# Feature chunks loaded by two transfers each, and the stores of split weight sums moved from SyncE's queue to GpSimd's

## The chip, the cores and the metric

One NeuronCore of a Trainium2 chip runs the whole program. The metric is the device time of one execution in microseconds (us): 3232.86 us is the median of three executions of the kernel before, which lie between 3230.33 and 3237.58 us.

## The reference

The input x is 2048 x 576, all in float32. The kernel computes

```
xn = layernorm(x)
s  = softmax_attention(xn @ wqkv, 32 heads of 18) @ wo
g  = silu( ((relu(x' @ W_gate)) * (x' @ W_up)) @ W_down )      # x' = xn, F = 4608
out = x + s * g
```

(in the code of the reference: `xn = _layernorm(x); s = _A_ref(xn, ...); g = _silu(_B_ref(xn, W_gate, W_up, W_down)); return x + s * g`). Products are made at nearly float32 accuracy: each operand is split into a high part (a float32r copy) and a low part (the difference), and three of the four part products are summed.

## The kernel before, in words

**Stages.** First a projection stage: the 2048 rows are taken in four groups of 512 (`g`), normalized, transposed to features, split into high and low parts, and multiplied with the weights of q, k and v. The results go to DRAM (`qd`, `kd`, `vd`). The split features go to DRAM too, as `xTd`, by `spill`. Then come 144 units: four row groups times 36 blocks of 128 of the 4608 hidden features. Unit `k` (function `emit_unit`) multiplies the 576 features of its row group with one gate and one up block (`up`, 27 steps of matmuls, tile `pg`). Steps of attention are woven between them: from unit 0 the row maxima (`pm`, reduced by VectorE on L272), from unit 16 also the exponentials (`psx`, then ScalarE). After every odd unit, 64 matmuls of `attend` (tile `po`) follow. After every even unit, `down` or `down_made` multiplies the hidden features of two units with the down weights (tile `py`). So work comes in pairs of units, and the groups of 64 `po` matmuls mark the pace. At last a stage projects with `wo` and writes the result.

**The features.** A chunk is 64 features x 512 rows as high and low parts. It stands twice in a tile of 128 partitions, on partitions 0 to 63 and on 64 to 127, because the gate product uses the lower and the up product the upper half of the array. The pool `xA` has nine buffers, one for each of the nine chunks of a group, so the next group's chunk can come only when the last unit of the present group (units 35, 71, 107) is done with that chunk. `load_x` (L298) loads one; `half` calls it after each chunk of these units, and the stage ahead calls it for group 0. Its DMA is issued on SyncE's queue (SP) and is pinned in program order there. Row loads of the weights (`rg`), of keys and queries (`kq`, `kA`, `qT`), the store of attention results (`od`) and others share SP's queue. In the units up to 17, SP's DMAs keep the program's order (`sp.kept`); after that a planner places them by its own estimates, except what is pinned.

**The sums of weight blocks.** From unit 36 on, the down product uses seven products of sums of blocks (as in Strassen's scheme), and these sums of the weights are made once, in units 1 to 35, and read back later (`load_w`, 378 loads of tile `w`). `make_items` builds, for each of 18 pairs of blocks, one load (`wp`) and seven items. An item has three parts: `start` adds two blocks into `wt` (VectorE in units 1 to 15, GpSimd after), `middle` copies it as the high part into `ws` on ScalarE (L773, `copy_now`), and `end` subtracts on GpSimd for the low part and stores the tile to `wtd`. `make_step` runs `end` of one item, `middle` of the next and `start` of a third. There are three such steps in each of the units 1 to 15 and five in each of the units 16 to 35. `ws` and `wt` have two buffers each, so ScalarE's copy of an item waits until the store of the item two before it has landed. ScalarE works in order: behind that copy stand the exponentials that free TensorE's banks.

**GpSimd's own order.** GpSimd (POOL; every instruction of it passes L88 and is kept in program order) also splits the gate and up weights of the next unit (`gw`, a copy and a subtraction), the down weights (`dw`), the hidden features (`hh`), and adds sums (`y`, `c`). In the kernel before it issues only the DMAs of `qd`, `kd`, `vd` in the first stage and of `gd` at the end of each group.

Of the kernel before, what the change touches and what calls it, by code (L numbers as in the profile page):

```python
# [9 lines left out]
F32 = mybir.dt.float32  # L10
# [9 lines left out]
def kernel(  # L20
# [10 lines left out]
    nc = tc.nc  # L31
    P = 128
    R = P // 2
# [39 lines left out]
    def vec(i):  # L73
        return tc.keep_in_program_order(i)

    pinned = tc.keep_in_program_order
# [28 lines left out]
    gp = Kept(nc.gpsimd)  # L105
    sp = Maybe(nc.sync, True)
# [13 lines left out]
    xTd = dram.tile([NQ, XC, P, 2 * 512], F32, name="xTd")  # L120
    gd = dram.tile([S, D], F32, name="gd")
    od = dram.tile([D, S], F32, name="od")
    wtd = dram.tile([NF // 2, 7, P, 2, HC], F32, name="wtd")
# [41 lines left out]
    def xtile(pl):  # L165
        return pl.tile([P, 2, 512], F32R, tag="x", name="x")
# [131 lines left out]

    def load_x(g, c):
        xc = xtile(xA)  # L300
        pinned(
            nc.sync.dma_start(
                xc.rearrange("p a s -> p (a s)").bitcast(F32),
                xTd[g, c // 2, c % 2 * R : c % 2 * R + R].unsqueeze(0).to_broadcast([2, R, 1024]),
            )
        )
        xcur.setdefault(g, []).append(xc)

    with ExitStack() as st:
# [293 lines left out]
        for g in range(NQ):  # L603
# [46 lines left out]
            if last:  # L650
# [17 lines left out]
                for c in range(KC - 2, KC):  # L668
                    load_x(0, c)
            else:  # L670
                for j in range(4):
                    v_job(wv, g, j)
                    if j == 0 and g == 0:
                        nxt = load_rows(g + 2)
                    if j == 1:
                        spill(g, marks[-1] if g == 0 else None)
                    if j and g == NQ - 2:
                        for c in range(3 * j - 3, min(3 * j, KC - 2)):
                            load_x(0, c)
# [28 lines left out]
    def up(k):  # L708

        g, f = units[k]  # L710
        gw = gus.pop(k)
        if k < N1 and (k % 2 == 0 or k == N1 - 1):
            ps = [psO.tile([P, 512], F32, name="po"), shared("pg2")]
        else:
            ps = [bank("pg0"), bank("pg1")]
        last = f == NF - 1 and k + 1 < len(units)
        xg = xcur[g]

        def ops(t, c, i, j, rows):
            return gw[rows, i, c, :], xg[c][rows, j, :]  # L720

        def half(t):
            for n, _ in enumerate(row_half(ps[t], ops, t)):
                c = n // len(PRODUCTS)
                if t and n % len(PRODUCTS) == 2:
                    if last:
                        load_x(units[k + 1][0], c)
                        if c == KC - 1:
                            load_up(k + 2)
                    elif k + 1 == len(units):  # L730
                        run_tasks(hooks.get(c, []))
                yield

        return ps, [half(t) for t in range(2)]
# [37 lines left out]
    def copy_now(dst, src):  # L772
        after(nc.scalar.activation(dst, src, AF.Copy), newest[0])  # L773
# [175 lines left out]
    def make_items(fp):  # L949

        st = {}

        def load():
            st["w"] = pw.tile([P, 2, D], F32, name="wp", bufs=1)
            for i in range(2):
                f = 2 * fp + i
                sp.dma_start(st["w"][:, i], wd[f * P : (f + 1) * P, :])

        def start(m, on):
            w = st["w"]  # L960
            b = [[w[:, i, c * HC : (c + 1) * HC] for c in range(2)] for i in range(2)]
            x0, x1, op = {
                0: (b[0][0], b[1][1], ALU.add), 1: (b[0][0], None, None), 2: (b[0][1], b[1][1], ALU.subtract),
                3: (b[1][0], b[0][0], ALU.subtract), 4: (b[1][1], None, None), 5: (b[0][0], b[0][1], ALU.add),
                6: (b[1][0], b[1][1], ALU.add),
            }[m]
            if op is not None:
                t = pw.tile([P, HC], F32, name="wt")
                if on is nc.vector:
                    vec(on.tensor_tensor(t, x0, x1, op))  # L970
                else:
                    gp.tensor_tensor(t, x0, x1, op)
                x0 = t
            st[m] = x0, pw.tile([P, 2, HC], F32R, name="ws")

        def middle(m):
            x0, s_ = st[m]
            copy_now(s_[:, 0], x0)

        def end(m):  # L980
            x0, s_ = st.pop(m)
            gp.tensor_tensor(s_[:, 1], x0, s_[:, 0].bitcast(F32), ALU.subtract)
            sp.dma_start(wtd[fp, m], s_.bitcast(F32))

        return [(load, start, middle, end, m) for m in (None, 1, 4, 0, 2, 3, 5, 6)]

    for fp in range(NF // 2):
# [432 lines left out]
```

## Time and profile before

| what | value |
|---|---|
| median of the three runs shown | 3232.86 us |
| time of the profiled execution | 3239.11 us |
| its span, first to last instruction | 3237.3 us |
| mean granted TensorE clock | 0.914 |
| TensorE busy | 2772.1 us (86%) |
| VectorE busy | 1867.7 us (58%) |
| ScalarE busy | 1665.0 us (51%) |
| GpSimd busy | 1746.8 us (54%) |
| SP's DMA queue | 350.43 MB, 37.6% of 16 engines |
| GpSimd's DMA queue | 27.66 MB, 2.5% of 16 engines |

The span and the busy times are of the one profiled execution; its own time is 1.8 us more than its span. A granted clock of 1.0 is 2.4 GHz and of 0.5 is 1.2 GHz. The chain of waits is followed back from the last instruction; here it reaches back to 683 us and not further, so the time before that is read from other views. "SPq" is SyncE's queue, and the time of a DMA there is that of its issue, not of its transfer.

### The profile page before, as it was taken

The page shows a single profiled execution, that of the slowest core. Times are in us where ns is not written, and L with a number is a line of the kernel's source. Part 1 is how long each engine was busy: PE and PEld are TensorE (multiplying, and loading weights), DVE is VectorE, ACT ScalarE, POOL GpSimd, SP SyncE. Part 2 cuts the span into 40 slices and gives each one's busy share as a digit, 9 for nine tenths or more (in the row PEclk, how much of TensorE's full clock was granted, in tenths as well). Part 3 has the DMA queues.
Part 4 walks back from the last instruction along what each step waited for, and adds up shares of the span by engine and source line. Part 5 has one row for each costly group of instructions (what it writes and reads, how often), then busy time and mean ns, then how long its engine had stood idle before and what let it go on. Part 6 is the DMA issues. An engine that isn't in the chain of part 4 may idle for free.

```text
span 3237.3 us, 63467 instructions
## 1 busy us (share of the span) xinstructions
PE 2772.1 (86%) x24653; PEld 2047.1 (63%) x24653; DVE 1867.7 (58%) x3118; ACT 1665.0 (51%) x3761; POOL 1746.8 (54%) x1762
## 2 busy tenths in 40 slices
PE   9967777787783799999992799999992799999999
PEld 8856665565662567767761567767771567766668
DVE  5233445554552577777771477777770577777315
ACT  3211114454442467767761467666671467767662
POOL 4225555555542465665650655656651665656667
PEclk9978878898886899999995899999995899999999
DMA  8454444344331433343331343443341334343346
GB/s 269 179 176 116 128 116 123 105 122 119 117 105 70 135 104 107 109 119 106 107 108 62 102 119 105 113 117 108 99 113 66 107 112 111 104 121 93 91 124 217
DMA packets 324979, 382.14 MB, mean 118 GB/s; under 512 B 33480, under 2 KB 214472, under 8 KB 324680
## 3 DMA queue, kind: packets, MB, share of 16 engines
q1 hardware_dynamic: 316936, 350.43, 37.6%
q0 software_dynamic: 7744, 27.66, 2.5%
q8 instruction: 195, 3.19, 0.4%
q14 instruction: 104, 0.85, 0.1%
HBM read 293.78 MB, written 83.69 MB: 117 GB/s over the span
## 4 chain that ended last, share of the span: by engine, by line
PE 54%; DMA 10%; POOL 7%; ACT 4%; issue 3%; SPq 1%; DVE 0%; POOLq 0%; ACTq 0%; DVEq 0%
PE pg L70 17%; PE po L70 11%; PE py L70 11%; PE pm L70 7%; PE psx L70 6%; DMA x<-xTd 6%; DMA wtd<-ws 2%; POOL gw L88 2%; PE pw L70 2%; POOL y L88 2%; ACT p L100 1%; SPq L100 1%; DMA rg<-in_B_W_up_dram 1%; ACT hc L773 1%; ACT hd L773 1%
## 5 line engine op out<-in xcount | busy, mean ns | idle before, releaser
L272 DVE TENSOR_REDUCE mx<-pm 128x1 f32<-128x512 f32 x2048 | 1345.0, 687 | 790.4 <-PE pm L70 647.3
L70 PE MATMUL pg<-x,gw 64*128 64x512 f32 x7533 | 1495.0, 410 | 171.8 <-DMA x<-xTd 153.4
L100 ACT ACTIVATE p<-psx 128x512 f32<-128x512 f32 x2048 | 1102.9, 615 | 405.7 <-PE psx L70 337.3
L70 PEld LDWEIGHTS pg<-x,gw 64*128 64x128 f32 x7533 | 1062.0, 195 | 302.8 <-DMA x<-xTd 165.9
L70 PE MATMUL po<-p,va 128*32 128x512 f32 x4096 | 454.3, 595 | 0.0
L88 POOL TENSOR_TENSOR gw<-rg,gw 128x1152 fp32r<-128x1152 f32 x131 | 349.4, 2667 | 10.5
L88 POOL TENSOR_TENSOR c<-add,c 128x288 f32<-128x288 f32 x204 | 157.8, 807 | 344.0 <-ACT add L890 344.0
L70 PEld LDWEIGHTS po<-p,va 128*32 128x32 f32 x4096 | 126.3, 110 | 294.8 <-issue 283.7
L70 PE MATMUL psx<-qT,kq 56*128 56x512 f32 x608 | 231.9, 410 | 33.9 <-ACT p L100 32.2
L70 PE MATMUL pm<-kq,qT 54*128 54x512 f32 x608 | 240.3, 417 | 19.1 <-ACT p L100 19.1
L70 PE MATMUL psx<-kq 56*128 56x512 f32 x512 | 199.7, 414 | 49.1 <-ACT p L100 47.6
L88 POOL CAST gw<-rg 128x1152 fp32r<-128x1152 f32 x131 | 150.7, 1151 | 168.3 <-PE pm L70 98.2
L88 POOL TENSOR_TENSOR hr<-h 128x256 f32<-128x256 f32 x108 | 79.4, 735 | 289.7 <-DVE nm L1099 151.0
L70 PE MATMUL pm<-kA,kq 54*128 54x512 f32 x512 | 207.2, 426 | 31.1 <-DMA kA<-kd 18.9
L70 PE MATMUL pm<-kq 54*128 54x512 f32 x512 | 207.2, 424 | 18.4 <-DVE mx L272 13.3
L70 PE MATMUL psx<-kq,kA 56*128 56x512 f32 x512 | 193.5, 406 | 20.5 <-ACT p L100 19.1
L70 PE MATMUL psx<-qT,kA 56*128 56x512 f32 x416 | 166.7, 423 | 45.2 <-ACT p L100 44.3
L70 PE MATMUL pm<-kA,qT 54*128 54x512 f32 x416 | 165.5, 422 | 12.6 <-ACT p L100 12.6
L742 DVE TENSOR_TENSOR h<-pg,h 128x512 f32<-128x512 f32 x144 | 98.1, 681 | 132.2 <-ACT h L100 132.2
L890 ACT ACTIVATE add<-py 128x288 f32<-128x288 f32 x357 | 141.3, 411 | 61.2 <-PE py L70 26.5
L773 ACT ACTIVATE ws<-wt 128x288 fp32r<-128x288 f32 x90 | 39.7, 442 | 254.3 <-DMA wtd<-ws 216.8
L70 PE MATMUL py<-dw,hh 64*128 64x288 f32 x1728 | 145.6, 327 | 25.9 <-DVE mx L272 12.9
(139 smaller groups left out, 4427.6 us busy)
## 6 DMA issues: line engine op xcount, KB each, us to landing
w<-wtd SPq DMA_DIRECT2D x378, 288.0 KB
rg<-in_B_W_gate_dram SPq DMA_DIRECT2D x131, 288.0 KB
rg<-in_B_W_up_dram SPq DMA_DIRECT2D x131, 288.0 KB
wtd<-ws SPq DMA_DIRECT2D x126, 288.0 KB
x<-xTd SPq DMA_DIRECT2D x36, 512.0 KB
rd<-in_B_W_down_dram SPq DMA_DIRECT2D x36, 288.0 KB
wp<-in_B_W_down_dram SPq DMA_DIRECT2D x36, 288.0 KB
qd<-hh POOLq DMA_DIRECT2D x16, 512.0 KB, 6.9
```

What stands on the lines that cost most here:

```text
L70: newest[0] = tc.keep_in_program_order(nc.tensor.matmul(*args, **kw))
L88: return lambda *args, **kw: tc.keep_in_program_order(op(*args, **kw))
L100: i = op(*args, **kw)
L272: vec(nc.vector.tensor_reduce(mx[:, h, b, j, c : c + 1], ps, axis=AX.X, op=ALU.max))
L742: vec(nc.vector.tensor_tensor(h, ps[1], h, ALU.mult))
L773: after(nc.scalar.activation(dst, src, AF.Copy), newest[0])
L890: pinned(nc.scalar.activation(src, outs_[p][j], AF.Copy))
```

## The change

Two edits. `load_x` issues two DMAs a chunk, each of which fills 64 partitions from the same block of `xTd`, where one DMA with a broadcast source of leading size 2 filled all 128. And `end` of an item stores its tile from GpSimd's queue in place of SP's.

```
     def load_x(g, c):
         xc = xtile(xA)
-        pinned(
-            nc.sync.dma_start(
-                xc.rearrange("p a s -> p (a s)").bitcast(F32),
-                xTd[g, c // 2, c % 2 * R : c % 2 * R + R].unsqueeze(0).to_broadcast([2, R, 1024]),
+        for t in range(2):
+            pinned(
+                nc.sync.dma_start(
+                    xc[t * R : (t + 1) * R].rearrange("p a s -> p (a s)").bitcast(F32),
+                    xTd[g, c // 2, c % 2 * R : c % 2 * R + R],
+                )
             )
-        )
         xcur.setdefault(g, []).append(xc)
...
         def end(m):
             x0, s_ = st.pop(m)
             gp.tensor_tensor(s_[:, 1], x0, s_[:, 0].bitcast(F32), ALU.subtract)
-            sp.dma_start(wtd[fp, m], s_.bitcast(F32))
+            gp.dma_start(wtd[fp, m], s_.bitcast(F32))
```

## Rows read from the trace of the kernel before

**Rows 1.** The page: TensorE's busy tenths in 40 slices of the span.
```profile
PE   9967777787783799999992799999992799999999
```
**Rows 2.** The chain of waits, in order of time: start us, us, what.
```profile
980.12 37.07 DMA wtd<-ws x2
1036.44 34.98 DMA x<-xTd
...
1696.49 56.86 DMA x<-xTd x2
...
2429.48 90.34 DMA x<-xTd x3
```
**Rows 3.** The waits, whole span: us in total, times, longest.
```profile
ACT ws L773 <- DMA wtd<-ws: 228.9, 49, 19.0
...
PE pg L70 <- DMA x<-xTd: 153.4, 19, 10.0
...
PE po L70 <- DMA x<-xTd: 17.7, 2, 9.9
```
**Rows 4.** Windows: length, busy us (instructions) by engine, granted clock, DMA share, GB/s.
```profile
2440.00:2450.00 10.00, 2.50 (x9) 1.48 (x9) 1.38 (x2) 1.01 (x2) 0.00 (x0) 0.50 0.13 52
1106.00:1107.00 1.00, 1.00 (x12) 0.82 (x9) 0.96 (x3) 1.00 (x3) 0.14 (x1) 1.00 0.95 273
...
180.00:220.00 40.00, 16.28 (x105) 13.70 (x107) 8.43 (x14) 2.43 (x7) 11.85 (x10) 0.62 0.57 171
```
**Rows 5.** TensorE in order of time: three `po` groups, units 31 to 37.
```profile
890.49 7.07 PE L70 MATMUL po<-p,va 128*32 128x512 f32 x64
940.67 7.07 PE L70 MATMUL po<-p,va 128*32 128x512 f32 x64
...
1095.15 7.07 PE L70 MATMUL po<-p,va 128*32 128x512 f32 x64
```
**Rows 6.** The chain of waits again: around units 71 and 107.
```profile
1658.24 7.00 PE po L70 x64
1676.12 6.66 PE py L70 x76
1693.34 3.15 PE po L70 x29
...
1827.57 7.06 PE po L70 x64
...
2425.96 3.52 PE po L70 x29
...
2555.36 7.00 PE po L70 x64
```
**Rows 7.** TensorE in order of time: where unit 73 begins.
```profile
1800.85 0.40 PE L70 MATMUL pg<-x,gw 64*128 64x512 f32 x1
```
**Rows 8.** SP's queue in order of time, behind the first seven loads of features.
```profile
157.41 21.29 SPq L100 DMA_DIRECT2D xTd<-x  x5
```
**Rows 9.** GpSimd in order of time: first weight split, and a `gd` store.
```profile
196.03 1.14 POOL L88 CAST gw<-rg 128x1152 fp32r<-128x1152 f32 x1 [25.06 <-DMA rg<-in_B_W_up_dram]
...
1093.77 0.62 POOL L88 DMA_DIRECT2D gd<-y  x1 [0.31 <-POOL y L88]
```
**Rows 10.** The tensor `gd`: time of its stores to landing.
```profile
DMA to landing us min/median/max: 2.4/2.7/6.2
```
**Rows 11.** The chain of waits once more: stores of `wtd`, and a load back.
```profile
787.50 0.33 SPq L100
...
789.24 4.14 DMA wtd<-ws
...
830.86 3.10 DMA wtd<-ws
...
1791.56 2.89 DMA w<-wtd
```
**Rows 12.** VectorE in order of time: row maxima back to back.
```profile
691.30 2.62 DVE L272 TENSOR_REDUCE mx<-pm 128x1 f32<-128x512 f32 x4 [0.46 <-PE psx L70]
```

## The prediction

> **What bounds the kernel now.** I read the page's slices first: TensorE is busy nine tenths or more through most of the second half, but there are three dips, at slices 13, 22 and 31 [rows 1]. These are where units 35, 71 and 107 hand over to the next row group. Between slices 3 and 13 it is at seven or eight tenths: that stage, units 1 to 35, is bound otherwise.
>
> The chain of waits says what the dips are: 34.98, 56.86 and 90.34 us of transfers `x<-xTd`, and ahead of the first 37.07 us of `wtd<-ws` [rows 2]. The list of waits agrees: TensorE itself waits 153.4 us for `x` in the units and 17.7 us more in unit 0 (whose gate product goes to a tile of the `po` pool), 171 us in all, and ScalarE waits 228.9 us for stores of `wtd` [rows 3].
>
> Then the windows: in the middle of a dip the DMA engines are 0.13 busy, which is two of sixteen, and move 52 GB/s [rows 4]. At that rate a chunk of 512 KB (524,288 bytes) takes 10.1 us and nine take 91 us, which is the 90.34 of the third dip. So the broadcast DMA, whose leading size is 2, runs on two engines. The granted clock there is 0.50 (1.2 GHz), after TensorE had little to do. In a microsecond with DMAs of 64 partitions each (the rows `rg`, beside `od`) in flight, the share is 0.95 and the rate 273 GB/s [rows 4]: a DMA over 64 partitions does spread.
>
> **Part one, two transfers a chunk.** Each of the 72 DMAs moves 256 KB over 64 partitions. At 273 GB/s a chunk takes 1.9 us and nine take 17 us; usual odd units give their nine buffers back over 10.6 us (1693.34 less 1676.12 and 6.66 [rows 6]), and then come 7.0 us of `po` before the next unit asks for its first chunk. So the chunks come in time, and what is late next is a load that waits its turn behind them: the weights for `down_made`, which arrive 2.89 us after their issue where TensorE waited for one [rows 11]. I leave 4 us at each handover for that and its issue. The 36 more issues cost nothing, as SP then waits for buffers and no longer for full rings; without that cover, 36 times a `gd`-like 0.62 us [rows 9] would be 22 us.
>
> The gain, place by place:
>
> - Units 71 to 73. From one `po` group to the next it is 134.2 us (1693.34 to 1827.57) where a usual pair takes 35.1 (1658.24 to 1693.34) [rows 6]. Of that, unit 73 has 26.7 us from its start at 1800.85 [rows 7] where an odd unit has 10.6; these 16.1 us are the sixteen additions of `combine` on GpSimd, which the change doesn't touch. 134.2 - 35.1 - 16.1 = 83, less 4: 79 us.
> - Units 107 to 109. In the same way 2555.36 - 2425.96 - 35.1 - 16.1 = 78 [rows 6], less 4: 74 us.
> - Units 34 to 37. 1095.15 - 940.67 = 154.5 us for two pairs [rows 5]. The first should take 50.2, as the pair before it. The second has no items any more, but the first sums of hidden features: between 35.1 and 50.2, and I take 41. Loss 63, less 4: 59 us. Here the stores that stood behind the loads in SP's order [rows 2] are counted too.
> - Unit 0: the 17.7 us of its wait [rows 3], say 18.
> - End of the first stage. From 180 to 220 us TensorE is busy 16.28 us at a mean clock of 0.62, about 10 us of work at full clock [rows 4], so 30 us are lost. Behind the seven loads SP takes 21.29 us to issue five spills, since the rings of two engines are full [rows 8]; behind these come the first weight rows, for which GpSimd waits 25.06 us at 196.03 [rows 9], and its stores of q and k stand behind that. I take 24 of the 30, as the last keys must still be stored and read back.
>
> Together 254 us. From below: only TensorE's own 171 us come back. From above: nothing is left late anywhere, 83 + 78 + 63 + 18 + 30 = 272.
>
> **Part two, the stores through GpSimd's queue.** A store of the same shape, 128 rows of 2304 bytes, stands in the trace: `gd`. Its issue holds GpSimd for 0.62 us, after 0.31 us of waiting for its own addition [rows 9]. So each of the 126 stores adds 0.93 us to GpSimd, 117 us in all. GpSimd is busy 54% of the span, and most of this falls into its idle time. What doesn't: after the weight split at a unit's start, GpSimd runs behind, and two items' subtractions come in a row, with the first item's store now between them. Behind that store stand the next `wt`, the next subtraction and, at the unit's end, the next weight split; for the second store ScalarE waits, and for ScalarE the exponentials and TensorE. One store of 0.93 us a unit, 35 units: 33 us.
>
> The landing: through SP 3.10 us from issue [rows 11]; through GpSimd 0.31 + 2.7 = 3.0 if the 2.7 [rows 10] count from the issue's start, 3.6 if from its end. Between nothing and 0.5 us a unit; I take the middle, 9 us. On the other side a store in SP waits its turn: the one at 789.24 was held since 787.50 by a load of `wp` [rows 11], 1.7 us. With one such in each of 17 pairs this returns 30 us. So part two costs 33 + 9 - 30 = 12 us. The ends are 117 us (every store on the path) and a gain of 30 (only the turns in SP count); 12 is nearer the second as the slack is wide.
>
> One rule speaks against this part. The row shows a GpSimd issue of 0.62 us in a stage in which VectorE works as well [rows 9]. The Trainium skill's page "SBUF — State Buffer" ("SBUF: two separate sides") warns that a DMA from GpSimd's queue needs GpSimd to write its descriptors, and that VectorE's fast float32 copies lock it out: 620 ns alone became about 3100 ns. By that, an estimate from the page, 126 x 2.5 = 312 us more would come and the kernel would be slower; by the row, nothing.
>
> **The sum.** The profiled execution took 3239.1 us. 3239.1 - 254 + 12 = 2997. That execution is 6.2 us above the median of the runs shown, so beside 3232.9 it is 2991 us.
>
> **The rivals**, all against the median:
>
> - Only the waits that carry the name `x` come back, since the places around them have other late loads (the weight rows, the queries, `w`). 3233 - 171 + 12 = 3074 us. For it: these loads share SP. Against it: they wait there because the `x` issues hold SP. 0.14.
> - GpSimd becomes the bound of units 1 to 35, and each store's 0.93 us counts. 3233 - 254 + 117 = 3096 us. For it: its work already stands on the chain there in bursts. Against it: it is idle nearly half the span. 0.13.
> - The stores help: ScalarE's waits shrink as the stores never wait in SP. 3233 - 272 - 30 = 2931 us. 0.07.
> - Slower: in units 1 to 35 GpSimd's issue of a store is held until VectorE's row of reduces ends. Four in a row are 2.62 us [rows 12]; 126 x (0.93 + 2.62) = 447, so 3233 - 254 + 447 = 3426 us. It decides from 254 / 126 = 2.0 us a store. Against it stands the 0.62 us of [rows 9]. 0.02. (The rule of the Trainium skill's "SBUF — State Buffer" would have it so for copies.)
> - The change doesn't do what it says: a DMA from one block of 256 KB doesn't spread, the nine chunks take 91 us again, and 12 us of part two and up to 22 of issues are added, 3245 to 3267 us. Against it the 0.95 share of [rows 4]. 0.04.
>
> **How the numbers follow.** My forecast has 0.60, its own range 2960 to 3030 us (part one between 225 and 272, part two between -10 and 45). The range for 8 in 10 is 2940 to 3080: it takes in the rival at 3074, part of that at 2931, and leaves out the two slower ones and most of that at 3096. A run of this kernel tells changes over 0.2% (6.5 us) from none. Faster: 0.60 + 0.14 + 0.13 + 0.07 = 0.94. Of the 0.04 for no spreading 0.01 lies within 0.2%, the rest with the 0.02 is slower: 0.05.
>
> **What would show it.** In the profile after, the dips in slices 13, 22 and 31 shrink to the 16 us of `combine`; `x<-xTd` leaves the list of TensorE's waits; the DMA share while chunks load is well above 0.13; from 180 to 220 us TensorE is busy. In units 16 to 35 a pair still takes 50 us, up to 52. Wrong would be: pairs of 55 us there (GpSimd is the bound), stores that hold GpSimd for over 1 us, a wait for `rg` or `w` of 10 us or more at a handover, or a share that stays at two engines.

## The result, and the profile after

The kernel with both edits takes 3031.21 us (median of three runs, 3031.11 to 3033.31) where the kernel before takes 3232.86: 201.6 us less, a ratio of 0.9376 (95% interval 0.9355 to 0.9397). The forecast was 2991 us with 2940 to 3080 as its range. The profiled execution took 3031.21 us, its span is 3029.4 us, the mean granted clock 0.946 (before 0.914), and TensorE is busy 90% of the span.

The page's slices for TensorE in the kernel after, in answer to [rows 1]: slice 3 is full now, the dips at units 71 and 107 are down to two eights (slices 22 and 23) and a seven (31), and slices 4 to 13, units 1 to 35, still show six and seven tenths.
```profile
PE   9996677777776999999998899999997999999999
```
The list of waits after (total us, times, longest), in answer to [rows 3]. TensorE no longer waits for `x`; one wait of ScalarE is left. ScalarE's wait for stores has grown from 228.9 to 245.7 us.
```profile
ACT ws L774 <- DMA wtd<-ws: 245.7, 44, 12.9
...
ACT ot L100 <- DMA x<-xTd: 6.8, 1, 6.8
```
Two windows after (columns as in [rows 4]). From 180 to 220 us TensorE had been busy 16.28 us at a clock of 0.62; now it is busy 39.67 of the 40 us, at a clock of 1.00 (2.4 GHz). While unit 71's chunks load, the share is about 1, all sixteen engines, at 253 GB/s, where it was 0.13 at 52 GB/s.
```profile
180.00:220.00 40.00, 39.67 (x416) 35.85 (x412) 27.16 (x43) 8.10 (x19) 19.71 (x21) 1.00 0.80 225
...
1610.00:1635.00 25.00, 24.89 (x210) 15.81 (x210) 17.76 (x30) 17.43 (x37) 8.45 (x8) 1.00 1.04 253
```
GpSimd's stores of `wtd` after, grouped by the tensor, in answer to [rows 9, 10]: 0.56 us each (557 to 582 ns), behind 0.32 us of waiting for the subtraction (39.9 us in 124 waits), and 2.9 us to landing.
```profile
L88 POOL DMA_DIRECT2D wtd<-ws x126: 557/560/582, 230.4 to 1007.7; - x126
...
  POOL ws L88: 39.9, 124
...
DMA to landing us min/median/max: 2.4/2.9/6.6
```
TensorE's `po` groups after, in order of time (start, duration), in answer to [rows 5, 6]: the first one (unit 17), those of units 33 and 37, and the two that bound units 72 and 73.
```profile
518.44 7.07 PE L70 MATMUL po<-p,va 128*32 128x512 f32 x64
...
928.23 7.07 PE L70 MATMUL po<-p,va 128*32 128x512 f32 x64
...
1020.50 7.65 PE L70 MATMUL po<-p,va 128*32 128x512 f32 x64
...
1619.42 7.07 PE L70 MATMUL po<-p,va 128*32 128x512 f32 x64
...
1684.73 7.07 PE L70 MATMUL po<-p,va 128*32 128x512 f32 x64
```
From such starts comes this table of stretches (us); the middle column is the first experiment below, with the edit of the feature loads alone.

| stretch, start of a `po` group to the next named | before | loads alone | both |
|---|---|---|---|
| start of the program to unit 17's | 542.3 | 494.1 | 518.4 |
| eight pairs, to unit 33's | 398.4 | 395.7 | 409.8 |
| two pairs, to unit 37's | 154.5 | 89.4 | 92.3 |
| the pair at units 72 and 73 | 134.2 | 66.7 | 65.3 |
| the pair at units 108 and 109 | 129.4 | 59.6 | 61.5 |

Nearly all that the loads give (250.6 of the table's 253.3 us) is in the first, third and last two lines. What the stores cost (24.3 us, 14.1 and 2.9, together 41.3) lies in units 1 to 37. At the two later handovers the last two columns differ by -1.4 and +1.9 us, and some 4 us of the 45.5 between the two spans (3029.4 - 2983.9) lie in parts that the table leaves out.

### The profile page after: what moved, and what is told of

Its sections match the earlier page's. It is cut to its first block, busy times and chain, and to the rows that moved or that the text cites. A ratio compares the mean times of both kernels' runs of the same rounds, so it can differ in the third digit from the quotient of the medians.

```text
span 3029.4 us, 63531 instructions
## 1 busy us (share of the span) xinstructions
PE 2739.4 (90%) x24653; PEld 2025.9 (67%) x24653; DVE 1863.7 (62%) x3118; ACT 1662.7 (55%) x3761; POOL 1822.1 (60%) x1888
## 4 chain that ended last, share of the span: by engine, by line
PE 68%; POOL 14%; DMA 6%; issue 5%; ACT 4%; DVE 1%; SPq 0%; POOLq 0%; ACTq 0%; DVEq 0%
PE pg L70 20%; PE py L70 14%; PE po L70 12%; PE pm L70 8%; PE psx L70 7%; POOL gw L88 5%; DMA wtd<-ws 4%; PE pq L70 3%; POOL dw L88 2%; PE pv L70 2%; POOL ws L88 2%; PE pw L70 2%; POOL y L88 2%; ACT p L100 1%; POOL hh L88 1%
## 5 line engine op out<-in xcount | busy, mean ns | idle before, releaser
L70 PE MATMUL pg<-x,gw 64*128 64x512 f32 x7533 | 1478.5, 406 | 11.7 <-DVE mx L272 11.7
L908 DVE TENSOR_TENSOR y<-py,y 128x288 f32<-128x288 f32 x255 | 112.0, 456 | 79.3 <-PE py L70 79.3
```

Of the source, the lines that this page charges most:

```text
L70: newest[0] = tc.keep_in_program_order(nc.tensor.matmul(*args, **kw))
L908: vec(nc.vector.tensor_tensor(dst, outs_[p][j], dst, ALU.add))
```

## The experiments

Medians with their lowest and highest run; ratios are against the kernel before on the same chip, whose medians there were 3230.26, 3229.41 and 3231.82 us, and 3232.86 beside the kernel after. Where medians from different chips are subtracted below, the ratios give a little less: the 44, 34, 10 and 23 us of this section are 40, 30, 10 and 21 by them.

**One edit each.** First the loads alone, the store left on SyncE's queue:
```
-            gp.dma_start(wtd[fp, m], s_.bitcast(F32))
+            sp.dma_start(wtd[fp, m], s_.bitcast(F32))
```


> Only the x edit; the stores stay in SP's queue. My theory: all of the gain is the spreading of x over sixteen engines, and the store edit costs. In the profile after, units 1 to 17 take 26.5 us longer and the next eight pairs 11.4 us longer than before, and I put this down to the store edit: 3031 - 26.5 - 11.4 = 2993, so 2985 to 3005 us, pairs of units 18 to 33 at 49.8 us again. Rival A: these units are slower because the x edit lets them begin before their weights are there; then this run is at 3025 to 3040. Rival B: the stores in SP's order get in the way of the fast loads at unit 35; then over 3040.

Measured: 2987.5 us (2985.67 to 2991.14), ratio 0.9252 (0.9238 to 0.9266). The spans of the two profiled executions differ by 3237.3 - 2983.9 = 253.4 us.

Then the stores alone, with the one broadcast DMA a chunk as in the kernel before:
```
-            sp.dma_start(wtd[fp, m], s_.bitcast(F32))
+            gp.dma_start(wtd[fp, m], s_.bitcast(F32))
```


> Only the store edit; x by one broadcast transfer a chunk. My theory: the store edit costs 38 us in units 1 to 33 and gives back at units 34 to 37 what the stores lost behind the x loads, at most 37 us: 3233 to 3271 us, pairs of units 18 to 33 at 51.4 us. Rival A (units 1 to 33 slow for the x edit): pairs at 49.8 us and 3195 to 3235 us in all.

Measured: 3272.7 us (3269.08 to 3273.78), ratio 1.0132 (1.0115 to 1.0149). So the loads return 243 us, the stores cost 42 without the loads' edit (1.3%, clear of the runs' scatter) and 3031.2 - 2987.5 = 44 with it; the two add up. The forecast's second part, 12 us, was too small by 32.

**Is it the two engines, or the number of transfers?** Two transfers a chunk, but each a broadcast of leading size 2 of half the columns:
```
+                    xc[:, t : t + 1].rearrange("p a s -> p (a s)").bitcast(F32),
+                    xTd[g, c // 2, c % 2 * R : c % 2 * R + R, t * 512 : t * 512 + 512].unsqueeze(0).to_broadcast([2, R, 512]),
```


> x by two transfers a chunk, but each still a broadcast of leading size 2 over all 128 partitions, of one half of the columns (2 KB runs); the stores stay in SP's queue. My theory: what counts is that the leading size of 2 confines a transfer to two engines, not the number of transfers: the DMA share while chunks load stays at 0.13 and the time at 3225 to 3260 us. Rival: two transfers in flight instead of one are what helps; then the share is about 0.25 and the time 3080 to 3150 us.

Measured: 3243.45 us (3238.03 to 3243.66), ratio 1.0039 (1.0024 to 1.0054). In its window in the third dip (columns as in [rows 4]) the share is 0.13 at 50 GB/s, as before.
```profile
2440.00:2450.00 10.00, 2.43 (x9) 1.52 (x10) 1.17 (x2) 1.01 (x2) 0.00 (x0) 0.50 0.13 50
```
Twice as many transfers return nothing (the time is 13 us longer); the leading size of 2 keeps them on two of the sixteen engines. This is what the Trainium skill's page "DMA: Bandwidth & Descriptors" ("Why a DMA increments its semaphore by 16 and not by 1") states: as many engines work as the largest number up to 16 that divides the slowest dimension above size 1 of both sides. The trace agrees, with 0.13 for 2 and about 1 for 64 partitions.

**What is late at a handover.** SP's queue around unit 72 in the kernel after (start, us, engine, line, DMA): nine chunks are 18 issues in a row, and the weights `rg` of the unit after next stand behind them.
```profile
1610.36 15.61 SPq L303 DMA_DIRECT2D x<-xTd  x18
1627.28 0.64 SPq L100 DMA_DIRECT2D rg<-in_B_W_gate_dram  x1
1628.31 0.62 SPq L100 DMA_DIRECT2D rg<-in_B_W_up_dram  x1
```
An issue takes 0.45 to 0.59 us, yet the 18 take 15.61. The waits of SP's queue from 1608 to 1632 us (total, times, longest) say why: ten of the issues wait for an earlier transfer of the same kind. These are the last ten; the trace's semaphore events show that SP's DMAs in this program take eight semaphores in turn, so that an issue waits until the transfer eight issues before it has landed.
```profile
SPq L303 <- DMA x<-xTd: 5.6, 10, 0.8
```
For them GpSimd waits 12.17 us; its row in order of time, the wait in brackets:
```profile
1636.63 1.15 POOL L88 CAST gw<-rg 128x1152 fp32r<-128x1152 f32 x1 [12.17 <-DMA rg<-in_B_W_up_dram]
```
On TensorE, behind that, a wait for GpSimd's sums `hd` follows, then one for a load of `w`, and then 13.32 us behind the sixteen additions of `combine`:
```profile
1643.05 0.61 PE L70 MATMUL py<-w,hd 64*128 64x288 f32 x2 [5.38 <-POOL hd L88]
...
1653.70 1.09 PE L70 MATMUL py<-w,hb 64*128 64x288 f32 x6 [5.55 <-DMA w<-wtd]
...
1680.39 0.79 PE L70 MATMUL psx<-qT,kq 56*128 56x512 f32 x1 [13.32 <-ACT p L100]
```
The next kernel has the loads' edit alone and issues these weights after the fourth chunk:
```
-                        if c == KC - 1:
+                        if c == 3:
                             load_up(k + 2)
```


> The x edit alone, and in units 35, 71 and 107 the weight rows of the unit after next (load_up) issued after the fourth chunk in place of the ninth. In the profile after, unit 72's split of the weights waits 12.2 us for these rows, and w stands behind them in SP's order; from one po group to the next there it is 65.4 us where 35.1 and 16.1 for combine would be 51.2. My theory: this wait is the 14 and 10 us that the two later handovers lack of my forecast; 15 to 25 us less than the run with the x edit alone, so 2965 to 2985. Rival: the loads are bound by the rate of the DMA engines there, all sixteen busy for 25 us; then the rows only change places with chunks, and within 5 us of the x edit alone.

Measured: 2975.6 us (2973.73 to 2977.88), ratio 0.9214 (0.9200 to 0.9228), 12 us less than the loads alone. GpSimd's wait there fell to 2.36 us:
```profile
1582.60 1.15 POOL L88 CAST gw<-rg 128x1152 fp32r<-128x1152 f32 x1 [2.36 <-DMA rg<-in_B_W_up_dram]
```
The pair at unit 72 takes 60.0 us in place of 66.7, that at 108 56.0 in place of 59.6. So `rg` behind the chunks was 10 us of the two handovers; a wait of 5.79 us for `w` on TensorE stays. The rival, that the rows would only change places with chunks, is refuted.

**Where the 44 us of the stores go.** The instruction streams of the two programs differ in more than the queue. The planner sets ScalarE's order by its own estimates, and the store's move alone places 43 of the 126 `ws` copies earlier among ScalarE's other instructions, by up to 15 places; the others keep their order, and TensorE's and VectorE's orders don't change. (In SP's queue 25 of the 1946 issues other than these stores stand elsewhere; this isn't followed up here.) In the next kernel, both edits are in, but ScalarE's order is forced to that of the loads alone:
```
-            copy_now(s_[:, 0], x0)
+            copies.append(copy_now(s_[:, 0], x0))
...
+    for n, name in behind.items():
+        tc.add_manual_dep(
+            copies[n].ins, f"I-{name}",
+            mybir.DependencyInfo(mybir.DependencyClass.NoSync, mybir.DependencyReason.DATA),
+            reason="order on ScalarE",
+        )
```
(`behind` names, for each of the 43 copies, the instruction that stands ahead of it with the loads alone; no wait is added, as both are ScalarE's.)

> Both edits, but with 43 of the 126 copies ws on ScalarE held back by order-only dependencies to the place they have with the x edit alone; without these the planner puts them up to 15 places earlier once the stores leave SP's queue, ahead of exponentials. The store edit costs 44 us on top of the x edit (3031 against 2987). My theory: 12 to 20 us of that are this new order (11 in units 15 and 16 alone), the rest is GpSimd's time: 3011 to 3020 us. Rival A, GpSimd's time alone: 3025 to 3035. Rival B, the order alone: 2984 to 2995.

Measured: 2997.34 us (2993.77 to 3000.76), ratio 0.9282 (0.9267 to 0.9297): 34 us less than with the planner's order, 10 us more than the loads alone. The order was worth more than expected, and lies nearer the rival that it is all. The converse: the loads alone, stores on SP, with those 43 copies forced early (22 of them not as far as in the kernel after, four of these not at all):
```
+    for n, name in ahead_of.items():
+        tc.add_manual_dep(
+            made_by[f"I-{name}"].ins, copies[n].ins.name,
+            mybir.DependencyInfo(mybir.DependencyClass.NoSync, mybir.DependencyReason.DATA),
+            reason="order on ScalarE",
+        )
```


> The converse of the run that forced the old order: the x edit alone, stores of wtd on SyncE's queue as before, but 43 of the 126 ws copies of ScalarE are forced ahead of the instructions that they precede when both edits are in (the first items of units 14 to 16 only some 7 places instead of 15). Theory: the earlier place of the copies costs by itself, since a copy that waits for the store two items before holds the exponentials behind it: 20 to 34 us above the x edit alone, 3008 to 3022 us. Rival: the early place costs only together with the stores in GpSimd's queue, which land later: at most 8 us above, 2980 to 2996 us.

Measured: 3010.84 us (3007.69 to 3012.91), ratio 0.9317 (0.93 to 0.9334), 23 us more than the loads alone. The order costs by itself, 23 to 34 us.

How it costs is seen on ScalarE in unit 16 of the kernel after (start, us, instruction, the wait before it in brackets): the copy that waits 6.89 us for a store stands ahead of exponentials whose products are ready.
```profile
470.52 0.58 ACT L100 ACTIVATE h<-po 128x512 f32<-128x512 f32 x1
...
475.86 1.09 ACT L100 ACTIVATE p<-psx 128x512 f32<-128x512 f32 x2 [0.23 <-PE psx L70]
483.84 0.44 ACT L774 ACTIVATE ws<-wt 128x288 fp32r<-128x288 f32 x1 [6.89 <-DMA wtd<-ws]
484.19 1.07 ACT L100 ACTIVATE p<-psx 128x512 f32<-128x512 f32 x2
...
492.66 0.60 ACT L100 ACTIVATE h<-pg 128x512 f32<-128x512 f32 x1 [0.27 <-PE pg L70]
```
TensorE in the same kernel waits for just these exponentials, which free its banks:
```profile
484.82 0.79 PE L70 MATMUL psx<-kq,kA 56*128 56x512 f32 x1 [6.45 <-ACT p L100]
```
The same stretch of ScalarE with the loads alone: nine exponentials run through, and the copy comes behind them, with a wait of 1.89 us.
```profile
452.58 0.58 ACT L100 ACTIVATE h<-po 128x512 f32<-128x512 f32 x1
...
459.80 5.04 ACT L100 ACTIVATE p<-psx 128x512 f32<-128x512 f32 x9 [0.41 <-PE psx L70]
465.13 0.60 ACT L100 ACTIVATE h<-pg 128x512 f32<-128x512 f32 x1 [0.29 <-PE pg L70]
...
472.33 0.44 ACT L773 ACTIVATE ws<-wt 128x288 fp32r<-128x288 f32 x1 [1.89 <-DMA wtd<-ws]
```
From `h<-po` to `h<-pg` it is 22.1 us in the one and 12.6 in the other. Not all of this difference stays: with the loads alone the copies come in the next unit, and up to the next `h<-pg` (518.11 and 494.61) it is 47.6 and 42.0 us.

The sum of ScalarE's waits for stores doesn't show this cost; where in the order a wait stands decides. With the loads alone it is
```profile
ACT ws L773 <- DMA wtd<-ws: 188.5, 49, 9.8
```
and with both edits in the old order, which takes 34 us less than the kernel after with its 245.7, it is
```profile
ACT ws L774 <- DMA wtd<-ws: 231.4, 56, 13.2
```

In unit 16 with the loads alone the store does stand in SP's order. The subtraction on GpSimd starts at 460.18 and takes 0.81 us:
```profile
460.18 0.81 POOL L88 TENSOR_TENSOR ws<-wt,ws 128x288 fp32r<-128x288 f32 x1
```
and SP issues the stores at 470.11, 9.1 us after its end, behind 20 loads of keys and queries:
```profile
461.09 4.49 SPq L100 DMA_DIRECT2D kq<-nr  x8
465.62 2.23 SPq L88 DMA_DIRECT2D qT<-qd  x6
467.89 2.11 SPq L88 DMA_DIRECT2D kA<-kd  x6
470.11 5.52 SPq L100 DMA_DIRECT2D wtd<-ws  x4
```
GpSimd's queue saves these 9 us, but most of them are worth nothing: the copy that needs the buffer stands behind the exponentials and waits only 1.89 us for it. With both edits and the old order the same copy, at 484.38, waits for nothing.

**Is it GpSimd's time?** Loads alone, stores on SP, and one more multiplication on GpSimd for each item, on a tile that nothing reads:
```
             gp.tensor_tensor(s_[:, 1], x0, s_[:, 0].bitcast(F32), ALU.subtract)
+            gp.tensor_tensor(junk, junk, junk, ALU.mult)
```


> The x edit alone, stores in SP's queue, but GpSimd does one more multiplication of a 128x288 scratch tile (about 0.87 us with its gap) behind each of the 126 subtractions, where the store edit puts 0.86 us of waiting and issuing. My theory: GpSimd's time itself is what costs, some 25 us: 3005 to 3020 us. Rival: the way of the store (its queue and landing) or the order on ScalarE costs, and GpSimd has room: 2982 to 2995.

Measured: 2985.29 us (2979.95 to 2988.93), ratio 0.9245 (0.9225 to 0.9266), no different from the loads alone. The theory on record is refuted and its rival holds. The group of these instructions (busy us, mean ns):
```profile
L88 POOL TENSOR_TENSOR junk<-junk 128x288 f32<-128x288 f32 x126 | 84.2, 668 | 0.0
```
So 0.67 us more on GpSimd for each item, right behind its subtraction, costs nothing; a store holds it for 0.88 us. (The store in SP's queue doesn't wait for this multiplication, so the run tests GpSimd's time and not a later store.)

**Does the cost go through ScalarE's wait for the buffer?** A third buffer of `ws` makes a copy wait for the store three items before, not two. It was tried with the loads alone, with the loads and the early `rg`, and with both edits of the change:
```
-            st[m] = x0, pw.tile([P, 2, HC], F32R, name="ws")
+            st[m] = x0, pw.tile([P, 2, HC], F32R, name="ws", bufs=3)
```


> The x edit alone, with three buffers for ws in place of two; the weight rows at their old place. Theory: the third buffer takes away most of ScalarE's wait for the store two items before, and the earlier weight rows of the other run are a separate 12 us: 2938 to 2948 us. Rival: the third buffer's gain needs the earlier rows or takes their gain with it: 2925 to 2935 us, or 2955 us and more.

> The run with early weight rows (2976), and a third buffer for ws, so that ScalarE's copy waits for the store three items before. Theory: ScalarE's 188 us of waits for stores are on the path in part: 2935 to 2965. Rival: GpSimd's bursts set the pace there whatever the buffers: 2970 to 2980.

> Both edits and a third buffer for ws. If the store edit's cost reaches TensorE by ScalarE's wait for the store two items before, the third buffer takes most of it away: 2975 to 3005 us. If it is GpSimd's time itself (the next weight split comes later): 3015 to 3030.

| third buffer, with | without it | with it | ratio with it |
|---|---|---|---|
| loads alone | 2987.5 | 2941.4 (2937.1 to 2945.52) | 0.9103 (0.9082 to 0.9125) |
| loads and early `rg` | 2975.6 | 2930.18 (2926.92 to 2932.24) | 0.9073 (0.9059 to 0.9088) |
| both edits | 3031.21 | 2946.95 (2945.62 to 2948.44) | 0.9126 (0.9113 to 0.9140) |

With three buffers the stores' queue makes a difference of 2947.0 - 2941.4 = 5.6 us, and the two intervals overlap. ScalarE's order is the planner's own in each, and it matters for the reading: with three buffers the planner places 41 copies of the loads alone early as well, so these two kernels differ less in order than the two with two buffers do. The plainer test is the kernel with both edits beside the same with a third buffer: GpSimd's and SP's orders are the same, ScalarE's copies stand at the same places or up to two places earlier (11 of 126), and yet the time is 84 us less, more than was expected. An early place costs only when the copy then waits for a store: the cost of the edit goes through that wait. The waits of ScalarE with both edits and three buffers, in answer to 245.7 us:
```profile
ACT ws L773 <- DMA wtd<-ws: 68.6, 18, 10.3
```
The kernel with the loads' edit, early `rg` and three buffers is the fastest here, 2930.2 - 3229.4 = -299 us beside the kernel before.

## Why the prediction was right, and which term was not

**Part one held in place and, in the sum, in size.** Forecast 254 us; between the profiled executions the loads alone return 253.4, by the medians 243 (the profiled execution of before lies 3239.1 - 3230.3 = 8.9 us above the median of before on that chip, and that of the loads alone 1.8 below its own). By place, from the table:

| place | forecast | loads alone |
|---|---|---|
| unit 0 and end of the first stage (with units 1 to 17) | 18 + 24 = 42 | 48.2 |
| units 18 to 33 | 0 | 2.7 |
| units 34 to 37 | 59 | 65.1 |
| units 71 to 73 | 79 | 67.5 |
| units 107 to 109 | 74 | 69.8 |

The premise that a DMA over 64 partitions spreads, read from one microsecond of [rows 4], is right. At the end of the first stage the five spills that took SP 21.29 us [rows 8] take 6.21 in the kernel after:
```profile
124.69 6.21 SPq L100 DMA_DIRECT2D xTd<-x  x5
```
So slow chunks held SP up there, as the forecast has it; that "the rings" were full is its explanation, and no view shows it. The 4 us left at a later handover were too few: beyond the usual 35.1 and the 16.1 of `combine`, 66.7 - 51.2 = 15.5 and 59.6 - 51.2 = 8.4 us stayed. The forecast named "a load that waits its turn behind them" and put it at the price of a load of `w`; what stood there was `rg`, behind 18 issues that took 15.61 us, and behind `rg` GpSimd's split and its sums `hd`. The forecast had nine chunks at 17 us of transfer right, and "the chunks come in time" too; it didn't carry those 17 us on to the loads that SP issues after them. "SP then waits for buffers" was too kind as well: ten of the 18 issues wait for earlier transfers. The places with more than forecast made up for it (48.2, 2.7 and 65.1 beside 42, 0 and 59): that the sum fits to a microsecond is luck.

**Part two was the step that failed:** 33 + 9 - 30 = 12 us forecast, 44 measured. These 32 us, with the 11 by which the loads' 243 fall short of 254 and less 3 between the medians of the kernel before, are the 40 by which 3031 lies above 2991; the range of 2940 to 3080 was wide enough for it. Term by term:

- "One store of 0.93 us a unit, 35 units: 33 us". The 0.93 us of [rows 9] is near, as the 126 stores hold GpSimd for 0.88 each, but the place on the path is not: 0.67 us more of GpSimd for each item cost nothing. (That was arithmetic in place of a DMA; a difference between the two isn't excluded by it.)
- "This returns 30 us", the turns in SP. The turns are there, 9.1 us in unit 16, but only a part comes back where the copy is placed behind other work, 1.89 us there. In no run is the store edit a gain over the whole; with the old order the eight pairs of units 18 to 33 are 5.3 us faster than with the loads alone, which may be these turns. The 1.7 us a turn was misread, too: the subtraction ahead of that store ends at 788.47, so the store issued at 789.24 was held for 0.77 us and not since 787.50:
```profile
787.67 0.80 POOL L88 TENSOR_TENSOR ws<-wt,ws 128x288 fp32r<-128x288 f32 x1 [0.20 <-ACT ws L773]
```
- "I take the middle, 9 us", the landing. What is left with the old order is 10 us. A unit ahead of unit 16 shows what such a step may be, in the same place of both programs. With both edits and the old order, the subtraction ends at 369.88, and the next copy starts at 373.12, 3.24 us later:
```profile
369.08 0.80 POOL L88 TENSOR_TENSOR ws<-wp,ws 128x288 fp32r<-128x288 f32 x1
370.64 0.56 POOL L88 DMA_DIRECT2D wtd<-ws  x1 [0.76 <-POOL ws L88]
...
373.12 0.44 ACT L774 ACTIVATE ws<-wt 128x288 fp32r<-128x288 f32 x1 [9.39 <-DMA wtd<-ws]
```
With the loads alone it ends at 360.90 and the copy starts at 363.16, after 2.26 us; SP takes the store 0.03 us after the subtraction:
```profile
360.11 0.79 POOL L88 TENSOR_TENSOR ws<-wp,ws 128x288 fp32r<-128x288 f32 x1
...
360.93 0.33 SPq L100 DMA_DIRECT2D wtd<-ws  x1
...
363.16 0.44 ACT L773 ACTIVATE ws<-wt 128x288 fp32r<-128x288 f32 x1 [8.31 <-DMA wtd<-ws]
```
That the 10 us are made of such steps is likely, since 15.1 us of it lie ahead of unit 17's `po` (509.2 against 494.1) and 5.3 us come back in the eight pairs; no run shows it.
- The term that was missing, 23 to 34 us: the forecast took ScalarE's order as given. That the planner places ScalarE's copies as well, and that a store in another queue pulls 43 of them ahead of exponentials, it did not weigh. (That the planner does so because it takes the store for done sooner is likely; no run shows its estimates.)

**The rivals.** "Only the waits that carry the name x" (171 us) is refuted by 243. "GpSimd becomes the bound" lies 65 us off (3096), and its cause is refuted: a pair in units 18 to 33 takes 409.8 / 8 = 51.2 us, where that rival needed 55, and more work on GpSimd cost nothing. The slower one fell with 126 issues of 557 to 582 ns: the lock that the Trainium skill's "SBUF — State Buffer" ("SBUF: two separate sides") warns of isn't seen here, though VectorE is busy three to five tenths of most slices in which they stand. Most of that work is row maxima and not the copies that the rule speaks of, so it is no test of the rule for copies. "The stores help" is refuted by the stores alone, 1.0132, and "doesn't spread" by the share of 1.04.

**The signs named beforehand.** `x<-xTd` left TensorE's waits, the share while chunks load is 1.04, and 180 to 220 us is full: as forecast. Pairs of "50 us, up to 52" in units 16 to 35: 51.2 in the mean of units 18 to 33, the longest 53.3. "A wait for `rg` or `w` of 10 us or more at a handover" was named as a sign of being wrong, and stands there with 12.17.

## What to carry to other kernels

Read a DMA's busy share: 0.13 is two engines of sixteen, and a leading broadcast of 2 puts it there whatever the number of transfers. When a store moves to another queue, look at what a planner then does with the order of the engine that waits for the store: here a copy that waited 6.89 us stood ahead of ready exponentials, while the store itself held its engine for 0.88 us. If a copy waits for the store two items before, try a third buffer first: it was worth 45 to 84 us here, more than the choice of the queue.

## What was not expected of the hardware

A store of 288 KB through GpSimd's queue (issue 0.56 us, landing 2.9 us in the median) is not much slower than through SP when SP is free: 0.98 us in the pair of places above. A row of long transfers holds SP at their own pace: from the eighth of the 18 transfers of 256 KB on it issues one every 1.05 us (1615.00 to 1625.52 in ten steps), which is 262,144 bytes / 1.05 us = 250 GB/s, the rate of the window at that time. This comes from the program's eight semaphores and isn't shown to be a limit of the queue itself. Either way a short load behind such a row is late by their transfer, not by their issues.
